# Turning expert and mix rows by VectorE in 32x32 blocks, from block-ordered loads, instead of by TensorE

## The chip, the core and the metric

The kernel runs on one core of one Trainium2 chip. A core has TensorE (PE, matrix products; its weight loads are shown as PEld), VectorE (DVE), ScalarE (ACT), GpSimd (POOL), SyncE (SP, which issues most DMAs here) and 16 DMA engines. The metric is the device time of one execution in microseconds, the median of the runs.

## What is computed

Input x has 4 sequences of 3072 rows of 256 numbers, 12288 rows (tokens) in all. Three stages follow one another:

```python
X = np.fft.fft(np.fft.fft(x, axis=1), axis=2).real        # 1. real part of a 2-D transform
x = X.reshape(12288, 256)

xn = x / (norm(x) + 1e-6); en = expert_emb / (norm(expert_emb) + 1e-6)
logits = xn @ en.T / tau                                   # 2. each row goes to one of 8 experts
e = argmax(logits); gate = softmax(logits)[e]
x = gate * (relu(x @ w1[e]) @ w2[e])                       # w1: 256x1024, w2: 1024x256

x_prev = x one row earlier in its sequence (zeros at its start)
xk = mu_k * x + (1 - mu_k) * x_prev; xr = mu_r * x + (1 - mu_r) * x_prev
k = relu(xk @ w_k)                                         # 3. mix; w_k: 256x1024
out = sigmoid(xr @ w_r) * ((k * k) @ w_v)                  # w_r: 256x256, w_v: 1024x256
```

## The kernel before

All matrix products of stages 2 and 3 run in three passes, since every operand is split into a high and a low part (`mm3`, L194): high by high, high by low, low by high. One product therefore shows three lines in the profile, L195, L196 and L197.

**Stage 1**, `transform_phase`, computes the transform and scatters each finished row to the DRAM tensor `xrows`, sorted by its expert: expert e owns rows from e * 12288 on. A row there is 272 numbers (1088 bytes): the 256 values, the token's number and its 8 logits. Stage 1 also works ahead on expert 0, whose first chunks are done there; a planner (`Plan`) orders that work by costs and due times. The change leaves stage 1 alone. At its end the rows of the first chunk of expert 1 are loaded already (`early_tiles`).

**Stage 2**, `expert_phase`, takes the rows of an expert in tiles of 128 rows and chunks of 4, 3, 3 and 3 tiles. It has 29 chunks: the last one of expert 0 (number `NP`) and four for each of experts 1 to 7. The loop over chunks is written out by hand; every engine runs its instructions in the order of the program and waits on semaphores. For chunk i the loop does this:

- `gather(i + 2)` (L1453) issues the row loads of the chunk after the next on SyncE, one DMA of 128 rows for each tile (`load_rows`, L235).
- `weigh(i)` lists the steps that give the gates and the destination of each row; these read the row tiles as they are loaded.
- For each of the 8 slices `fc` of the hidden layer: `first_layer(i, fc)` multiplies w1 by the turned rows (6 matmuls of 384 or 512 columns into one of two PSUM banks "a"), ScalarE evicts the high part (L1270), VectorE the low part (L1271, `hl`); then some weight splitting (L1177 on ScalarE, L1180 on VectorE; the wide weights of stage 3 at L1216 to L1242); then `second_layer(i - 1, fc)` for the chunk before (3 matmuls of 256 columns for each tile).
- At `fc == 3`, `transposes(i + 1)` (L1456) turns the next chunk's rows so that the 256 values lie on partitions: `transpose_chunk` (L1310) lets TensorE transpose each 128x128 block against the identity into PSUM (L1316), ScalarE copies the high part `th` (L1317), VectorE subtracts for the low part `tl` (L1318).
- At the end `finish(i - 1)` scales the chunk's results into tiles `y` (L1498) and GpSimd scatters them to the DRAM tensor `ydram` in token order (L178).

The loads of the raw weights, 1 MB each (`expert_raw`, L1164), go through the same SyncE queue.

**Stage 3**, `mix_phase`, runs over 24 blocks j of 512 tokens. `load(j)` (L1586) fetches a block from `ydram` with one DMA of 512 KB in runs of 1 KB, three buffers deep. `prepare(j + 1)` spreads the next block's preparation over the steps `fc` of block j: in steps 0 and 1 `turn(0)` and `turn(1)` (L1606) turn one half of the 256 values each (four TensorE transposes, L1609, and a ScalarE copy, L1610); in steps 2 to 6 `begin` and `end` form the two mixtures (L1617, L1618, L1624, L1625). Step fc of block j is, in this order: `key_layer(j, fc)` (6 matmuls of 512 columns, then L1661 on ScalarE and L1663 on VectorE); the second half of the previous step's squares (`late`: L1669 on ScalarE, L1670 `hl` on VectorE); a gate tile in steps 4 to 7; one step of `prepare`; and `value_layer` of two steps before (12 matmuls of 256 columns). When that was a block's last value layer, `finish` multiplies its four results in PSUM with the gates (L1701, `ot`, VectorE), which frees the four PSUM banks "b", and stores the block. So `finish(j - 1)` stands in step 1 of block j, behind `turn(1)`, and the value layer that opens the new block's sums in those banks stands in step 2.

At the start of stage 3 three blocks are loaded at once, while TensorE still does the second layer of the last chunk of stage 2.

Of the kernel before, what the change touches and what calls it, by code (L numbers as in the profile page):

```python
# [10 lines left out]
F32 = mybir.dt.float32  # L11
# [4 lines left out]
ACTF = mybir.ActivationFunctionType  # L16
ALU = mybir.AluOpType
# [4 lines left out]
D = 256  # L22
E = 8
F = 1024
NTOK = NB * S
# [20 lines left out]
NP = len(FIRST_CHUNKS) - 1  # L46
# [188 lines left out]
def load_rows(g, e, o, n, later=()):  # L235

    tiles = []
    for t in range(o, o + n):
        x = g.xg.tile([128, ROW], F32, tag="xg", name="xg")
        r = e * NTOK + 128 * t  # L240
        ins = g.nc.sync.dma_start(out=x, in_=g.xrows[r:r + 128]).ins
        for other in later:
            g.tc.declare_no_dep(ins, other, reason="rows of later ranks")
        g.row_reads.append(ins)
        tiles.append(x)
    return tiles
# [914 lines left out]
def expert_raw(g, e, n):  # L1161
    raw = g.xs.tile([128, 2048], F32, tag="xs", name="wraw")
    src = g.aps[n][e].rearrange("(k p) f -> p k f", p=128)
    g.nc.sync.dma_start(out=raw.rearrange("p (k f) -> p k f", k=src.shape[1]), in_=src)  # L1164
    return raw


def split_steps(g, raw, width=512, pool="w8"):

    nc = g.nc  # L1170
    hi, lo = [(g.w8 if pool == "w8" else g.xs).tile([128, 2048], F32R, tag=pool, name=n) for n in ("wh", "wl")]

    def piece(o):
        def fn():
            if o < 2048:
                s = slice(o, o + width)
                nc.scalar.activation(out=hi[:, s], in_=raw[:, s], func=ACTF.Copy)  # L1177
            if o:
                s = slice(o - width, o)
                nc.vector.tensor_tensor(out=lo[:, s], in0=raw[:, s], in1=hi[:, s].bitcast(F32), op=ALU.subtract)  # L1180
        return fn

    return (hi, lo), [piece(o) for o in range(0, 2049, width)]
# [123 lines left out]
    ]  # L1307


def transpose_chunk(g, tiles, ntile, dst_h, dst_l, tag="c"):  # L1310
    nc = g.nc
    for k in range(2):
        pt = g.ps.tile([128, 512], F32, tag=tag, bufs=g.banks[tag], name="pt")
        n = ntile * 128
        for t in range(ntile):
            nc.tensor.transpose(pt[:, t * 128:(t + 1) * 128], tiles[t][:, k * 128:(k + 1) * 128], g.ident)  # L1316
        nc.scalar.activation(out=dst_h[:, k, 0:n], in_=pt[:, 0:n], func=ACTF.Copy)  # L1317
        nc.vector.tensor_tensor(out=dst_l[:, k, 0:n], in0=pt[:, 0:n], in1=dst_h[:, k, 0:n].bitcast(F32),  # L1318
                                op=ALU.subtract)


def overflow_table(g, p2):
# [113 lines left out]
def expert_phase(g):  # L1436
    nc, tc = g.nc, g.tc
    a = g.aps
# [1 line left out]
    g.ps = g.ctx.enter_context(tc.tile_pool(name="ps", bufs=2, space=bass.MemoryType.PSUM))  # L1440
    g.banks = {"a": 2, "b": 4, "c": 2}
    xt_p = g.right.enter_context(tc.tile_pool(name="xt", bufs=2, side="right"))
    g.y = g.ctx.enter_context(tc.tile_pool(name="y", bufs=6))
    g.xs = g.inner.enter_context(tc.tile_pool(name="xsp", bufs=3))
    p2 = ctx.enter_context(tc.tile_pool(name="p2", bufs=1))
    y_p = g.y
# [3 lines left out]
    allc = [(0, o, n) for o, n, _ in FIRST_CHUNKS] + [(e, o, n) for e in range(1, E) for o, n in CHUNKS]  # L1450
    tiles, xts = g.early_tiles, {NP: g.early_x}

    def gather(i):  # L1453
        tiles[i] = load_rows(g, *allc[i])

    def transposes(i):  # L1456
        n = allc[i][2]
        th = xt_p.tile([128, 2, 512], F32R, tag="th", name="th")
        tl = xt_p.tile([128, 2, 512], F32R, tag="tl", name="tl")
        transpose_chunk(g, tiles[i], n, th, tl)  # L1460
        xts[i] = th, tl

    w = {0: list(g.w_first)}
# [38 lines left out]
    raws[1, 0] = expert_raw(g, 1, "w1")  # L1502
    for i, n in enumerate(("mu_k", "mu_r")):
        nc.sync.dma_start(out=g.mu[:, i, :], in_=a[n].rearrange("(k p) -> p k", p=128))
    for i in range(NP, n_all - 1):
        e, o, n = allc[i]
        if i == NP + 2:
            g.m2, wide = wide_weight_steps(g, cv_p)
        if i == NP + 1:
            overflow_table(g, p2)  # L1510
            nc.vector.tensor_scalar(out=g.omu, in0=g.mu, scalar1=-1.0, scalar2=1.0, op0=ALU.mult, op1=ALU.add)
        if i + 2 < n_all:
            gather(i + 2)

        c = (i - NP - 1) % len(CHUNKS) if e else 1
        if c == 0:
            second, fill = split_steps(g, raws[e, 1], pool="w8" if e + 1 < E else "xs")
            w[e].append(second)
            if e + 1 < E:
                raws[e + 1, 0] = expert_raw(g, e + 1, "w1")  # L1520
        if c == 1 and e + 1 < E:
            raws[e + 1, 1] = expert_raw(g, e + 1, "w2")
            first, fill = split_steps(g, raws[e + 1, 0])
            w[e + 1] = [first]
        weigh(i)
        for fc in range(8):
            first_layer(i, fc)
            for _ in range(-(-len(weighs) // (8 - fc))):
                weighs.pop(0)()
            if fc in (1, 3, 5, 6, 7) and fill:  # L1530
                fill.pop(0)()
            for _ in range(1 + (fc % 3 == 0)):
                if wide:
                    wide.pop(0)()
            if i > NP:
                second_layer(i - 1, fc)
            if fc == 3 and i + 1 < n_all:
                transposes(i + 1)
        if i > NP:
            finish(i - 1)  # L1540
# [32 lines left out]
def mix_phase(g):  # L1573
    nc, tc = g.nc, g.tc
    a = g.aps
    ctx = g.right
    yl_p = ctx.enter_context(tc.tile_pool(name="yl", bufs=3, side="right"))
# [6 lines left out]
    ld, yts, mixed = {}, {}, {}  # L1584

    def load(j):  # L1586
        t = yl_p.tile([128, 4, D], F32, tag="yl", name="yl")
        nc.sync.dma_start(out=t, in_=g.ydram[j * 512:(j + 1) * 512].rearrange("(t p) d -> p t d", p=128))
        ld[j] = t

    def prepare(j):

        yt = yt_p.tile([128, 2, 516], F32, tag="yt", name="yt")
        t = ld.pop(j)
        yts[j] = yt
        prev = yts.pop(j - 1, None)
        res = [[mx_p.tile([128, 2, 512], F32R, tag=f"m{q}{m}", name="mix") for q in range(2)] for m in range(2)]
        mixed[j] = res

        def halo():  # L1600
            if j % (S // 512) == 0:
                nc.vector.memset(yt[:, :, 3:4], 0.0)
            else:
                nc.vector.tensor_copy(out=yt[:, :, 3:4], in_=prev[:, :, 515:516])

        def turn(k):  # L1606
            pt = g.ps.tile([128, 512], F32, tag="c", bufs=2, name="pt")
            for s in range(4):
                nc.tensor.transpose(pt[:, s * 128:(s + 1) * 128], t[:, s, k * 128:(k + 1) * 128], g.ident)  # L1609
            nc.scalar.activation(out=yt[:, k, 4:516], in_=pt, func=ACTF.Copy)  # L1610

        tms = {}

        def begin(m, k):
            tm = mx_p.tile([128, 512], F32, tag="tm", name="tm")
            tms[m, k] = tm
            nc.scalar.activation(out=tm, in_=yt[:, k, 3:515], func=ACTF.Copy, scale=omu[:, m, k:k + 1])  # L1617
            nc.vector.scalar_tensor_tensor(out=tm, in0=yt[:, k, 4:516], scalar=mu[:, m, k:k + 1],  # L1618
                                           in1=tm, op0=ALU.mult, op1=ALU.add)

        def end(m, k):
            hi, lo = res[m]
            tm = tms.pop((m, k))
            nc.scalar.activation(out=hi[:, k], in_=tm, func=ACTF.Copy)  # L1624
            nc.vector.tensor_tensor(out=lo[:, k], in0=tm, in1=hi[:, k].bitcast(F32), op=ALU.subtract)  # L1625

        qs = [(0, 0), (0, 1), (1, 0), (1, 1)]

        def slot(i):
            def fn():  # L1630
                if i == 0:
                    halo()
                if i < 2:
                    turn(i)
                if 3 <= i < 7:
                    end(*qs[i - 3])
                if 2 <= i < 6:
                    begin(*qs[i - 2])
            return fn

        if j:
            return [slot(i) for i in range(7)]
        return [
            lambda: (halo(), turn(0)),
            lambda: (begin(*qs[0]), turn(1)),
            lambda: (end(*qs[0]), begin(*qs[1])),
            lambda: (end(*qs[1]), begin(*qs[2])),
            lambda: (end(*qs[2]), begin(*qs[3])),
            lambda: end(*qs[3]),
        ]  # L1650
# [54 lines left out]
    for j in range(3):  # L1705
        load(j)
# [5 lines left out]
    for at in range(8 * NBLK):  # L1712
        j, fc = divmod(at, 8)
# [12 lines left out]
        if at >= LAG:  # L1726
            k, kc = divmod(at - LAG, 8)
# [160 lines left out]
```

## Time and profile before

| | before |
|---|---|
| median of 3 runs (lowest to highest) | 1419.52 us (1418.83 to 1420.88) |
| profiled execution: its time, and its span | 1421.69 us, 1419.9 us |
| TensorE (PE) busy | 1357.0 us, 96% |
| weight loads (PEld) busy | 1268.2 us, 89% |
| VectorE (DVE) busy | 833.8 us, 59% |
| ScalarE (ACT) busy | 757.0 us, 53% |
| GpSimd (POOL) busy | 278.9 us, 20% |
| DMA | 75947 packets, 105.12 MB, mean 74 GB/s |

The page of the profile cuts the span into 40 equal slices of 35.5 us and gives each engine's busy share in tenths (9 is 90% or more):

```profile
PE   4768998999999999999999999999999999999998
DVE  8685346555555555554332666666666666666664
ACT  2445545545455555455544665566565565565563
PEclk9879999999999999999999999999999999999999
DMA  9843336123213131322102111110010111110000
```

The first six or seven slices are stage 1, the next fifteen stage 2 (from about 230 us), the rest stage 3 (from about 775 us). PEclk is the clock granted to TensorE, in tenths of full speed. Matmuls are pipelined, so their durations overlap: what one costs in a stream is seen from the distance between starts, not from its duration. In the timeline, a line's bracket holds the idle time of its engine just before it and who ended it.

### The profile page before, as it was taken

How to read it: one execution, taken by the hardware profiler on the slowest of the kernel's cores; microseconds unless marked ns; L12 is line 12 of the kernel's file. 1: busy time of each engine (PE TensorE's matmuls, PEld its weight loads, DVE VectorE, ACT ScalarE, POOL GpSimd, SP SyncE). 2: the span in 40 equal slices, each digit the busy share in tenths (PEclk: the TensorE clock that was granted, in tenths of full speed). 3: DMA queues.
4: the chain of work that ended last, by engine and by line, in shares of the span. 5: the costliest groups of instructions: out<-in, count | busy, mean ns of one | idle time of the engine just before them, and what ended most of it. 6: DMA issues, size and time to landing. Idle time of an engine off the chain costs nothing. (4 is left out here: it accounts for less than half of the span.)

```text
span 1419.9 us, 24364 instructions
## 1 busy us (share of the span) xinstructions
PE 1357.0 (96%) x9252; PEld 1268.2 (89%) x9252; DVE 833.8 (59%) x1905; ACT 757.0 (53%) x1888; POOL 278.9 (20%) x275
## 2 busy tenths in 40 slices
PE   4768998999999999999999999999999999999998
PEld 3657897999999999999999899999999999999998
DVE  8685346555555555554332666666666666666664
ACT  2445545545455555455544665566565565565563
POOL 5677673122222221222221000000000000000000
PEclk9879999999999999999999999999999999999999
DMA  9843336123213131322102111110010111110000
GB/s 287 195 132 111 115 108 196 69 80 108 80 62 126 53 99 57 98 76 80 47 23 68 39 60 31 30 60 30 31 60 30 44 47 30 56 35 31 30 16 30
DMA packets 75947, 105.12 MB, mean 74 GB/s; under 512 B 7694, under 2 KB 65331, under 8 KB 75188
## 3 DMA queue, kind: packets, MB, share of 16 engines
q1 hardware_dynamic: 61148, 72.74, 16.2%
q0 software_dynamic: 14352, 30.69, 7.1%
q8 instruction: 73, 1.20, 0.4%
q14 instruction: 46, 0.38, 0.1%
q10 hardware_dynamic: 328, 0.12, 0.0%
HBM read 62.73 MB, written 41.81 MB: 74 GB/s over the span
## 5 line engine op out<-in xcount | busy, mean ns | idle before, releaser
L1271 DVE SCALAR_TENSOR_TENSOR hl<-ph,hh 128x384 fp32r<-128x384 f32 (+1 forms) x232 | 136.6, 590 | 238.3 <-ACT hh L1270 237.2
L1663 DVE SCALAR_TENSOR_TENSOR k<-ph,r 128x512 f32<-128x512 f32 x192 | 132.8, 692 | 221.0 <-ACT r L1661 221.0
L1661 ACT ACTIVATE r<-ph 128x512 f32<-128x512 f32 x192 | 114.9, 598 | 257.4 <-PE ph L197 257.4
L1270 ACT ACTIVATE hh<-ph 128x384 fp32r<-128x384 f32 (+1 forms) x232 | 119.9, 517 | 238.9 <-PE ph L197 238.8
L195 PE MATMUL po<-wv,hh 128*128 128x256 f32 x768 | 219.6, 286 | 0.7 <-ACT hh L1669 0.7
L197 PE MATMUL po<-wv,hl 128*128 128x256 f32 x768 | 216.8, 282 | 0.4 <-DVE hl L1670 0.4
L196 PE MATMUL po<-wv,hh 128*128 128x256 f32 x768 | 215.3, 280 | 0.0
L195 PE MATMUL po<-wh,hh 128*128 128x256 f32 x752 | 211.4, 281 | 2.0 <-DVEq L1380 2.0
L197 PE MATMUL po<-wh,hl 128*128 128x256 f32 x752 | 211.0, 281 | 0.0
L196 PE MATMUL po<-wl,hh 128*128 128x256 f32 x752 | 210.6, 280 | 0.0
L178 POOL DMA_INDIRECT ydram<-y,ids x94 | 94.8, 1008 | 409.9 <-DVE ids L264 263.4
L195 PE MATMUL ph<-th,wh 128*128 128x384 f32 (+1 forms) x448 | 158.9, 355 | 0.7 <-DVE hl L1271 0.6
L197 PE MATMUL ph<-th,wl 128*128 128x384 f32 (+1 forms) x448 | 157.1, 351 | 0.0
L196 PE MATMUL ph<-tl,wh 128*128 128x384 f32 (+1 forms) x448 | 156.7, 350 | 0.0
L195 PE MATMUL ph<-mix,wk 128*128 128x512 f32 x384 | 151.7, 395 | 0.0
L196 PE MATMUL ph<-mix,wk 128*128 128x512 f32 x384 | 151.5, 394 | 0.0
L197 PE MATMUL ph<-mix,wk 128*128 128x512 f32 x384 | 151.4, 394 | 0.0
L195 PEld LDWEIGHTS po<-wv,hh 128*128 128x128 f32 x768 | 144.4, 188 | 3.2 <-ACT hh L1669 0.9
L196 PEld LDWEIGHTS po<-wv,hh 128*128 128x128 f32 x768 | 144.7, 188 | 2.2
L195 PEld LDWEIGHTS po<-wh,hh 128*128 128x128 f32 x752 | 142.1, 189 | 4.7 <-issue 2.3
L197 PEld LDWEIGHTS po<-wv,hl 128*128 128x128 f32 x768 | 144.5, 188 | 0.6 <-DVE hl L1670 0.6
L196 PEld LDWEIGHTS po<-wl,hh 128*128 128x128 f32 x752 | 142.3, 189 | 2.7
(262 smaller groups left out, 2974.8 us busy)
## 6 DMA issues: line engine op xcount, KB each, us to landing
wraw<-in_w_dram SPq DMA_DIRECT2D x16, 1024.0 KB
xg<-xrows SPq DMA_DIRECT2D x104, 136.0 KB
yl<-ydram SPq DMA_DIRECT2D x24, 512.0 KB
out_dram<-ot SPq DMA_DIRECT2D x23, 512.0 KB
xs<-in_xg_dram SPq DMA_DIRECT2D x9, 512.0 KB
xs<-in_xg_dram POOLq DMA_DIRECT2D x9, 512.0 KB, 7.4
xs<-in_xg_dram SPq DMA_DIRECT2D x3, 1024.0 KB
xrows<-zero SPq DMA_DIRECT2D x2, 1088.0 KB
```

The source lines that it names most:

```text
L178: ins = g.nc.gpsimd.indirect_dma_start(in_offset=None, oob_is_err=False, **kw).ins
L195: nc.tensor.matmul(out=out, lhsT=ah, rhs=bh, start=first, stop=False)
L196: nc.tensor.matmul(out=out, lhsT=ah, rhs=bl, start=False, stop=False)
L197: nc.tensor.matmul(out=out, lhsT=al, rhs=bh, start=False, stop=last)
L1270: return (lambda: nc.scalar.activation(out=hh[:, 0:N], in_=ps[:, 0:N], func=ACTF.Relu), lambda: nc.vector.scalar_tensor_tensor(out=hl[:, 0 ...
L1271: lambda: nc.vector.scalar_tensor_tensor(out=hl[:, 0:N], in0=ps[:, 0:N], scalar=0.0, in1=hh[:, 0:N].bitcast(F32), op0=ALU.max, op1=ALU.sub ...
L1661: nc.scalar.activation(out=r, in_=ps, func=ACTF.Relu)
L1663: nc.vector.scalar_tensor_tensor(out=k2, in0=ps, scalar=0.0, in1=r, op0=ALU.max, op1=ALU.mult)
```

## The change

Row loads for turning are made a second time, in the order of 32x32 blocks: `load_blocks` issues, for each half k of the 256 values and each group q of 32 partitions, one DMA on SyncE, whose runs are 32 numbers (128 bytes). Partition 32q + p of the result holds, for each group of 32 rows, 32 consecutive values of its p-th row; VectorE's transpose of 32x32 blocks then gives the turned rows at once. In stage 2 the old row loads stay, since gates and destinations are read from them; the blocks come beside them, into the new pool `xb` (two buffers, and one tile `xT` for the turned rows). The rows of chunk NP + 1, loaded in stage 1, get only their blocks, at the start of stage 2. ScalarE and VectorE then read `xT` in SBUF in place of PSUM. In stage 3 the block load takes the place of the old load, and VectorE's transpose takes the place of four TensorE transposes and a ScalarE copy. Expert 0's chunks, turned in stage 1, stay as they were. The pool `y` goes from six buffers to four.

```diff
-def transpose_chunk(g, tiles, ntile, dst_h, dst_l, tag="c"):
-    nc = g.nc
+def load_blocks(nc, out, rows):
+
+    n, step = rows.shape[0], rows.ap[0][0]
     for k in range(2):
-        pt = g.ps.tile([128, 512], F32, tag=tag, bufs=g.banks[tag], name="pt")
-        n = ntile * 128
-        for t in range(ntile):
-            nc.tensor.transpose(pt[:, t * 128:(t + 1) * 128], tiles[t][:, k * 128:(k + 1) * 128], g.ident)
-        nc.scalar.activation(out=dst_h[:, k, 0:n], in_=pt[:, 0:n], func=ACTF.Copy)
-        nc.vector.tensor_tensor(out=dst_l[:, k, 0:n], in0=pt[:, 0:n], in1=dst_h[:, k, 0:n].bitcast(F32),
-                                op=ALU.subtract)
+        for q in range(4):
+            src = bass.AP(rows.tensor, rows.offset + 128 * k + 32 * q, [[step, 32], [32 * step, n // 32], [1, 32]])
+            nc.sync.dma_start(out=out[32 * q:32 * q + 32, k, 0:n].rearrange("p (a j) -> p a j", j=32), in_=src)
 
@@ expert_phase
-    g.y = g.ctx.enter_context(tc.tile_pool(name="y", bufs=6))
+    xb_p = g.right.enter_context(tc.tile_pool(name="xb", bufs=2, side="right"))
+    g.y = g.ctx.enter_context(tc.tile_pool(name="y", bufs=4))
 
-    def gather(i):
-        tiles[i] = load_rows(g, *allc[i])
+    blocks = {}
+
+    def gather(i, here=False):
+        e, o, n = allc[i]
+        if not here:
+            tiles[i] = load_rows(g, e, o, n)
+        blocks[i] = xb_p.tile([128, 2, 512], F32, tag="xb", name="xb")
+        r = e * NTOK + 128 * o
+        load_blocks(nc, blocks[i], g.xrows[r:r + 128 * n, 0:D])
 
     def transposes(i):
-        n = allc[i][2]
+        N = allc[i][2] * 128
         th = xt_p.tile([128, 2, 512], F32R, tag="th", name="th")
         tl = xt_p.tile([128, 2, 512], F32R, tag="tl", name="tl")
-        transpose_chunk(g, tiles[i], n, th, tl)
+        x, xb = xb_p.tile([128, 2, 512], F32, tag="xT", bufs=1, name="xT"), blocks.pop(i)
+        for k in range(2):
+            nc.vector.transpose(out=x[:, k, 0:N], in_=xb[:, k, 0:N])
+            nc.scalar.activation(out=th[:, k, 0:N], in_=x[:, k, 0:N], func=ACTF.Copy)
+        for k in range(2):
+            nc.vector.tensor_tensor(out=tl[:, k, 0:N], in0=x[:, k, 0:N], in1=th[:, k, 0:N].bitcast(F32),
+                                    op=ALU.subtract)
         xts[i] = th, tl
 
@@ expert_phase, ahead of the loop over chunks
+    gather(NP + 1, True)
     for i in range(NP, n_all - 1):
 
@@ mix_phase
     def load(j):
-        t = yl_p.tile([128, 4, D], F32, tag="yl", name="yl")
-        nc.sync.dma_start(out=t, in_=g.ydram[j * 512:(j + 1) * 512].rearrange("(t p) d -> p t d", p=128))
+        t = yl_p.tile([128, 2, 512], F32, tag="yl", name="yl")
+        load_blocks(nc, t, g.ydram[j * 512:(j + 1) * 512])
         ld[j] = t
 
         def turn(k):
-            pt = g.ps.tile([128, 512], F32, tag="c", bufs=2, name="pt")
-            for s in range(4):
-                nc.tensor.transpose(pt[:, s * 128:(s + 1) * 128], t[:, s, k * 128:(k + 1) * 128], g.ident)
-            nc.scalar.activation(out=yt[:, k, 4:516], in_=pt, func=ACTF.Copy)
+            nc.vector.transpose(out=yt[:, k, 4:516], in_=t[:, k])
```

## Rows read from the trace of the kernel before

**Rows 1.** Windows: busy us (xcount) of each engine, TensorE clock, DMA share, GB/s.

```profile
265.00:490.00 225.00, 224.76 (x1580) 218.24 (x1579) 124.56 (x343) 116.81 (x346) 49.57 (x51) 1.00 0.26 83
...
800.00:1400.00 600.00, 600.00 (x4020) 548.28 (x4019) 390.29 (x663) 353.48 (x683) 0.00 (x0) 1.00 0.12 38
```

**Rows 2.** Lines view, TensorE transposes: xcount | busy us, mean ns | idle before.

```profile
L1609 PE MATMUL pt<-pack,yl 128*128 128x128 f32 x192 | 28.7, 271 | 0.0
...
L1316 PE MATMUL pt<-pack,xg 128*128 128x128 f32 x182 | 24.4, 272 | 0.0
```

**Rows 3.** Timeline, mix, without and with a group: start us, us, engine line.

```profile
1001.73 0.39 PE L197 MATMUL ph<-mix,wk 128*128 128x512 f32 x1
...
1002.08 0.28 PE L196 MATMUL po<-wv,hh 128*128 128x256 f32 x1
...
1021.49 0.39 PE L197 MATMUL ph<-mix,wk 128*128 128x512 f32 x1
1021.72 0.60 PE L1609 MATMUL pt<-pack,yl 128*128 128x128 f32 x4
...
1022.28 0.28 PE L196 MATMUL po<-wv,hh 128*128 128x256 f32 x1
```

**Rows 4.** Timeline, TensorE, expert chunk, without and with a group.

```profile
497.78 0.28 PE L197 MATMUL po<-wh,hl 128*128 128x256 f32 x1
...
498.07 0.34 PE L196 MATMUL ph<-tl,wh 128*128 128x384 f32 x1
...
500.23 0.28 PE L197 MATMUL po<-wh,hl 128*128 128x256 f32 x1
500.35 0.82 PE L1316 MATMUL pt<-pack,xg 128*128 128x128 f32 x6
...
501.18 0.34 PE L196 MATMUL ph<-tl,wh 128*128 128x384 f32 x1
```

**Rows 5.** Source view, VectorE, 1024 columns: duration ns min/median/max.

```profile
L455 DVE TENSOR_TENSOR xs<-xs x3: 1217/1225/1225, 33.3 to 95.4; 128x1024 f32<-128x1024 f32 x3
```

**Rows 6.** Lines view, VectorE, nearest shapes in SBUF.

```profile
L1625 DVE TENSOR_TENSOR mix<-tm,mix 128x512 fp32r<-128x512 f32 x96 | 66.4, 691 | 3.7 <-ACT mix L1624 2.1
...
L1222 DVE TENSOR_SCALAR fb<-ab 128x256 int32<-128x256 int32 x18 | 5.5, 305 | 0.0
```

**Rows 7.** Timeline, VectorE, mix, second step of a block.

```profile
1026.46 0.68 DVE L1670 TENSOR_TENSOR hl<-k,hh 128x512 fp32r<-128x512 f32 x1
1027.06 1.41 DVE L1701 TENSOR_TENSOR ot<-po,sg 128x256 f32<-128x256 f32 x4
```

**Rows 8.** Source view, VectorE, output products: duration ns min/median/max.

```profile
L1701 DVE TENSOR_TENSOR ot<-po,sg x96: 412/416/425, 817.0 to 1416.3; 128x256 f32<-128x256 f32 x96
```

**Rows 9.** Timeline, TensorE, mix, first value matmul of the next step.

```profile
1028.22 0.28 PE L195 MATMUL po<-wv,hh 128*128 128x256 f32 x1
```

**Rows 10.** Timeline, VectorE and TensorE, around one expert chunk's transposes.

```profile
500.94 0.29 DVE L1222 TENSOR_SCALAR fb<-ab 128x256 int32<-128x256 int32 x1
...
505.90 0.34 PE L195 MATMUL ph<-th,wh 128*128 128x384 f32 x1
```

**Rows 11.** Windows view: the first three mix loads, 1 KB runs.

```profile
775.00:780.00 5.00, 5.00 (x32) 5.00 (x32) 0.06 (x1) 1.19 (x3) 0.00 (x0) 0.66 0.91 303
```

**Rows 12.** Timeline, SyncE's queue, start of the expert phase.

```profile
230.58 1.80 SPq L241 DMA_DIRECT2D xg<-xrows  x3
```

**Rows 13.** Timeline, ScalarE and TensorE, start of the expert phase.

```profile
235.13 0.63 ACT L1177 ACTIVATE wh<-wraw 128x512 fp32r<-128x512 f32 x1 [1.82 <-DMA wraw<-in_w_dram]
...
240.30 0.44 PE L195 MATMUL ph<-xT,wfirst 128*128 128x384 f32 x1 [1.15 <-DVE hl L1271]
```

**Rows 14.** Timeline, SyncE, TensorE, ScalarE, start of the mix.

```profile
773.60 0.39 SPq L1588 DMA_DIRECT2D yl<-ydram  x1
...
774.13 0.38 PE L195 MATMUL po<-wh,hh 128*128 128x256 f32 x1 [1.99 <-DVEq L1380]
...
781.12 0.60 ACT L1610 ACTIVATE yt<-pt 128x512 f32<-128x512 f32 x1 [0.17 <-PE pt L1609]
```

## The prediction

> **What bounds the kernel now.** I read the windows view first, one stretch of the expert phase and one of the mix, to see which engine has no gap. In both it is TensorE: 224.76 of 225 us and 600.00 of 600 us busy at the full granted clock, where VectorE is busy 55% and 65% and the DMA engines 26% and 12% [rows 1]. So a microsecond of TensorE work that goes is a microsecond of the span, until another engine makes TensorE wait. Then the lines view, for what is to be removed: 192 transposes in the mix and 182 in the experts, with no idle time before them [rows 2]. Their mean of 271 ns is not their price, since matmuls overlap; the price comes from the distance between their neighbours' starts in the timeline.
>
> **Part 1, the transposes leave TensorE.** In the mix the last key matmul and the second value matmul behind it start 0.35 us apart without a group of four transposes (1001.73, 1002.08) and 0.79 us apart with one (1021.49, 1022.28): 0.44 us a group [rows 3]. There are 192/4 = 48 groups: 21.1 us. In an expert chunk of three tiles the same distance is 0.29 us without (497.78, 498.07) and 0.95 us with six (500.23, 501.18): 0.66 us, 0.11 each [rows 4]. Of the 182 I leave out the 8 of the first turned chunk, where TensorE waits for others anyway (part 4): 174 x 0.11 = 19.1 us. Together 40.2 us.
>
> **Part 2, the mix: VectorE turns.** ScalarE loses its copy out of PSUM, VectorE gets two 128x512 transposes a block. The trace has none, so its price is bounded by rows: at most the 1.22 us of a sum over twice the columns [rows 5], at least the 0.305 us of the cheap form over half of them. I take 0.69 us, the ordinary pass over 512 columns in SBUF [rows 6], which holds VectorE 0.60 us before the next starts [rows 7].
> The Trainium skill, VectorE: DVE Perf Modes, section The three transpose paths, gives 390 ns for TensorE and 311 ns for VectorE per 128x128 (bf16), and its rules for authors send a 128x128 transpose to TensorE. An estimate from that page, four times 311 ns for 512 columns, is 1.24 us, at the upper end above; in this trace TensorE pays 0.11 us in the stream instead of 390 ns, so the rule's comparison is still more against the change.
> Where does it stand? turn(0) falls into a step where VectorE waits anyway. turn(1) falls into the second step of a block, between hl and the four output products of the block before (L1701), which free the banks that the next block's first value matmul needs. In the profile ot starts at 1027.06 [rows 7] and its first quarter takes 0.416 us [rows 8]: done at 1027.48. The value matmul starts at 1028.22 [rows 9] and comes 0.44 us earlier once the transposes just ahead of it are gone: 1027.78. Cover 0.30 us; 0.05 of it, an estimate, goes to the signal between the engines. The transpose takes 0.60 us, and its four DMA waits (one for each group of partitions) I put at 0.10 (between 0 and 0.2). So TensorE waits 0.60 + 0.10 - 0.25 = 0.45 us in 22 blocks (those that hold both a finish and a turn): +9.9 us. At the lower end of the transpose (0.22 + 0.10 - 0.25) it is 1.6 us, at the upper (1.14 + 0.10 - 0.25) 21.8 us.
>
> **Part 3, expert chunks in their steady part: nothing.** VectorE gets two transposes more a chunk, and ScalarE's copies, the later eviction and its subtraction queue behind them. Cover: in the chunk shown VectorE is free at 501.23 [rows 10]; two turns, a copy, an eviction and its subtraction at 384 columns, each three quarters of 0.69 [rows 6], end 2.6 us later at 503.8; TensorE needs that bank at 505.90 less 0.66 = 505.24 [rows 4, 10]. 1.4 us are left; at the upper end of the transpose the cover is about used up, and then each chunk loses some tenths. y with four buffers instead of six still holds one chunk's tiles.
>
> **Part 4, the loads.** Each tile of 512 KB now comes in 4096 runs of 128 bytes, 256 a DMA engine, issued as 8 DMAs, beside the row loads that stay for the experts. The nearest row is the mix's first three loads in 1 KB runs: 5.0 us at a share of 0.91 for 1536 runs, 96 an engine: 47 ns each [rows 11]. An eighth of that, by bytes alone, is 6 ns. SyncE needs 0.39 to 0.60 us per DMA [rows 12, 14], which for its 32 runs an engine is 12 to 19 ns, so less can't arrive in a burst. I take 20 ns. Steady need: 13 tiles x 64 = 832 runs an engine per expert, 17 us (39 at 47 ns) beside 0.26 of some 75 us (225 us of rows 1 hold three experts); in the mix 5 us (12) of 25. SyncE's eight issues, about 4 us, are queued ahead of the weight loads and behind the output store; buffers come free one to two chunks ahead. Covered, cost 0.
> Not covered is the start of the experts. The first turned chunk's rows were loaded early; its blocks are issued only where the phase begins, behind 1 MB of weights, in the place where row loads stood at 230.58 [rows 12]. Those weights are there at 235.13 [rows 13]. The blocks follow: 256 x 0.020 = 5.1, 240.2; then the turn 0.69, ScalarE's copy 0.60, a subtraction 0.69 and the waiting eviction's subtraction, 384 columns, 0.5: 242.7. TensorE resumes at 240.30 [rows 13], so +2.4. Its gap then grows from 1.15 to 3.5 us. What a gap can do is seen at the mix: after 1.99 us idle [rows 14] the granted clock is 0.66 over the next 5 us, that is part of them at 1.2 GHz [rows 11], 1.7 us of work lost; I add these: +4.1. At 47 ns it is 2.4 + 6.9 + 1.7 = 11.0; at 6 ns about 0.
> At the start of the mix load(0) is issued at 773.60 and the second turned half is ready at 781.12 + 0.60 = 781.72, having waited 0.17 us for TensorE [rows 14], whose transposes stand behind value matmuls there: the load is not the last to come, by how much no row shows. Its runs take 5.1 us an engine instead of 32 x 0.047 = 1.5, so the half comes between 0 and 3.6 us later; I take 1.0, since the load goes out while TensorE still has work, and the 0.88 us of the first two groups is then not felt: +1.9. At 47 ns (12.0 instead of 5.1) +8.8.
>
> **Sum.** The profiled execution took 1421.69 us, 2.17 above the median. 1421.7 - 40.2 + 9.9 + 4.1 + 1.9 = 1397.4; less 2.2, 1395 us beside a median of 1419.5.
>
> **Rivals.** (a) Nothing of parts 2 and 4 is felt: 1421.7 - 40.2 - 2.2 = 1379. For it: VectorE idles a third of the mix; against: that idle time isn't ahead of ot. (b) The transpose takes 1.22 us: 9.9 becomes 21.8, 1407. For it: nothing in the trace shows its speed. (c) A 128-byte run costs what 1 KB does: 6.9 more at either start, 1409. (d) Both (b) and (c): 1421, no change. (e) Slower: the DMA engines become the bound. Expert phase: 832 runs x t + 20 us exceed 75.5 - 2.9 = 72.6 from t = 63 ns on (mix: from about 90). At t = 75 ns an expert takes 82 us, 7 x 9.4 = 66 us more, and the starts 14 each: 1489. Against it: 47 ns for eight times the bytes. The Trainium skill, DMA: Bandwidth & Descriptors, section Specifications, speaks for (c) and (e): full rate needs 512 bytes, below it a read-modify-write is done. No row here shows that. (f) That a transpose stays on TensorE can't be, outside expert 0: no such instruction is left in the diff.
>
> **How the numbers follow.** Forecast 53%, (a) 12, (b) 10, (c) 9, (d) 6, (e) 10. The range goes from (a), 1379, to just past (b) and (c), 1412, and leaves out (d) and (e). A measurement here tells 0.2% from no change: faster is the forecast, (a), (b), (c), 84%; same (d), 6%; slower (e), 10%.
>
> **What would show it.** No TensorE transposes behind the start of the experts; mix blocks 0.4 us shorter, not 0.9, with one TensorE wait a block on ot at L1701's place; a VectorE transpose near 0.69 us; expert chunks shorter by 0.11 us a transpose; one gap of some 3.5 us in the first chunk. The forecast is wrong if the turn waits for its DMAs in the steady part, if the ot wait is absent, or if the transpose is far from 0.69 us.

## The result, and the profile after

The changed kernel takes 1397.53 us (median of 4 runs, 1396.48 to 1398.58) where the kernel before takes 1420.17 on the same chip: a ratio of 0.9842, 95% interval 0.9825 to 0.9859. The forecast was 1395, range 1379 to 1412. Its profiled execution took 1397.23 us, span 1395.5.

First the page: busy time of each engine, and the first DMA queue (packets, MB, share of 16 engines).

```profile
PE 1322.6 (95%) x8878; PEld 1227.9 (88%) x8878; DVE 887.7 (64%) x2009; ACT 734.1 (53%) x1840; POOL 277.0 (20%) x275
...
q1 hardware_dynamic: 246620, 84.69, 25.1%
```

TensorE works 34 us less and the span is 24 us shorter; the difference is new waiting. Where it is not, the windows view shows (columns as in [rows 1]):

```profile
265.00:490.00 225.00, 224.86 (x1564) 218.34 (x1564) 141.17 (x385) 123.32 (x363) 54.37 (x55) 1.00 0.43 114
...
800.00:1280.00 480.00, 474.84 (x3109) 428.90 (x3110) 337.76 (x576) 270.93 (x521) 0.00 (x0) 1.00 0.20 43
```

The steady experts stay without a gap, though the DMA engines went from a share of 0.26 to 0.43. The mix, without a gap in [rows 1], now has 5.2 us of them in 480. The waits view of TensorE from 790 to 1395 us (total us, times, longest) names their cause, and it is the only one there:

```profile
PE po L195 <- DVE ot L1710: 6.2, 22, 0.5
```

The new instruction in the lines view of VectorE (xcount | busy, mean ns | idle before), and for the experts in the source view (min/median/max ns):

```profile
L1619 DVE STREAM_TRANSPOSE yt<-yl 128x512 f32<-128x512 f32 x48 | 33.8, 705 | 2.8 <-DMA yl<-ydram 2.8
```
```profile
L1467 DVE STREAM_TRANSPOSE xT<-xb x56: 532/570/712, 236.6 to 730.1; 128x384 f32<-128x384 f32 x42, 128x512 f32<-128x512 f32 x14
```

One 128x512 transpose takes 0.705 us, about what the ordinary pass of [rows 6] takes. One wait in front of it is long, at the first mix block.

The place in the loop, in the timeline: VectorE and then TensorE, step 1 into step 2 of a mix block (compare [rows 7, 3]).

```profile
1006.06 0.68 DVE L1679 TENSOR_TENSOR hl<-k,hh 128x512 fp32r<-128x512 f32 x1
1006.66 0.70 DVE L1619 STREAM_TRANSPOSE yt<-yl 128x512 f32<-128x512 f32 x1
1007.29 1.38 DVE L1710 TENSOR_TENSOR ot<-po,sg 128x256 f32<-128x256 f32 x4
```
```profile
1007.16 0.40 PE L197 MATMUL ph<-mix,wk 128*128 128x512 f32 x1
1007.82 0.36 PE L195 MATMUL po<-wv,hh 128*128 128x256 f32 x1 [0.27 <-DVE ot L1710]
1008.02 0.28 PE L196 MATMUL po<-wv,hh 128*128 128x256 f32 x1
```

The transpose sits between hl and the four products and holds VectorE for 0.63 us (1006.66 to 1007.29). From the last key matmul to the second value matmul it is now 0.86 us instead of the 0.35 of [rows 3]. What a block takes is seen at its store; the first and the twentieth store on SyncE's queue, of the kernel before and then of the changed one:

```profile
818.47 0.38 SPq L1703 DMA_DIRECT2D out_dram<-ot  x1
...
1317.29 0.38 SPq L1703 DMA_DIRECT2D out_dram<-ot  x1
```
```profile
800.94 0.41 SPq L1712 DMA_DIRECT2D out_dram<-ot  x1
...
1293.96 0.40 SPq L1712 DMA_DIRECT2D out_dram<-ot  x1
```

Over 19 blocks that is 26.254 us a block before and 25.948 after: 0.305 less, not the 0.88 of two groups of transposes.

The start of the experts, in the timeline of SyncE, ScalarE, VectorE and TensorE (compare [rows 12, 13]):

```profile
227.40 0.38 SPq L1164 DMA_DIRECT2D wraw<-in_w_dram  x1
...
228.88 7.62 SPq L1316 DMA_DIRECT2D xb<-xrows  x8
```
```profile
236.60 0.71 DVE L1467 STREAM_TRANSPOSE xT<-xb 128x512 f32<-128x512 f32 x1 [0.40 <-DMA xb<-xrows]
238.64 0.71 DVE L1467 STREAM_TRANSPOSE xT<-xb 128x512 f32<-128x512 f32 x1 [1.33 <-DMA xb<-xrows]
...
241.27 0.69 PE L195 MATMUL ph<-xT,wfirst 128*128 128x384 f32 x1 [3.96 <-DVE hl L1271]
...
244.81 0.42 PE L195 MATMUL ph<-th,wh 128*128 128x512 f32 x1
```

The gap that was 1.15 us is 3.96 us; its releaser hl stands on VectorE behind the two transposes, which waited for their blocks, and the two subtractions `tl`.

Cut into stretches, the two traces say: from the first matmul of the chunk `NP`, behind a wait of 0.75 us on ScalarE in both (229.71 before, 228.08 after), to the first turned chunk's first matmul (242.80, 244.81) +3.64 us; from there to the mix's first load (773.60, 756.54) -19.07; from there to the end -7.34. Together -22.8, beside -22.6 of the medians. Ahead of the first stretch the profiled execution was also 1.63 us earlier, in work that the change doesn't touch.

### The profile page after: what moved, and what is told of

The parts are those of the page before. It is cut to its first block, busy times and chain, and to the rows that moved or that the text cites. A ratio compares the mean times of both kernels' runs of the same rounds, so it can differ in the third digit from the quotient of the medians.

```text
span 1395.5 us, 24153 instructions
## 1 busy us (share of the span) xinstructions
PE 1322.6 (95%) x8878; PEld 1227.9 (88%) x8878; DVE 887.7 (64%) x2009; ACT 734.1 (53%) x1840; POOL 277.0 (20%) x275
## 3 DMA queue, kind: packets, MB, share of 16 engines
q8 instruction: 70, 1.15, 0.3%
```

## The experiments

My theory: the mix loses the 0.575 us a block (0.88 less 0.305) because turn(1) is queued ahead of the products ot, and the start of the experts loses its 3.6 us because the block loads come late. The rivals: the loads in 128-byte runs cost this time, or VectorE's greater load as such.

**1. Both transposes in step 0.**

```diff
-                if i < 2:
-                    turn(i)
+                if i == 0:
+                    turn(0)
+                    turn(1)
```

> Both transposes of a mix block stand in step 0 of the block before it; step 1, where the four products ot of the block before are made, has none. Theory A (what the mix still loses is the second transpose, which stands on VectorE ahead of the four products that TensorE waits for): the wait of TensorE on ot, some 0.5 us in 22 blocks, goes, a block falls from 25.95 to about 25.4 us, and the time from 1397.5 to about 1386 us. Theory B (the loss comes from the loads in runs of 128 bytes, or from VectorE's larger load as such): both are as they were, so the block stays within 0.1 us of 25.95 and the time within 2 us of 1397.5.

Measured: 1389.46 us, ratio 0.9784 (0.9766 to 0.9801). The wait on ot is gone from the waits view. SyncE's first and twentieth store, then VectorE and TensorE where the 0.86 us stood:

```profile
803.87 0.40 SPq L1713 DMA_DIRECT2D out_dram<-ot  x1
...
1287.11 0.39 SPq L1713 DMA_DIRECT2D out_dram<-ot  x1
```
```profile
1005.35 0.68 DVE L1680 TENSOR_TENSOR hl<-k,hh 128x512 fp32r<-128x512 f32 x1
1005.95 1.41 DVE L1711 TENSOR_TENSOR ot<-po,sg 128x256 f32<-128x256 f32 x4
...
1006.45 0.42 PE L197 MATMUL ph<-mix,wk 128*128 128x512 f32 x1
1006.70 0.29 PE L195 MATMUL po<-wv,hh 128*128 128x256 f32 x1
1006.82 0.28 PE L196 MATMUL po<-wv,hh 128*128 128x256 f32 x1
```

25.434 us a block, 0.514 less, and 0.37 us from matmul to matmul: theory A. The whole time fell by 8 us rather than the 11 expected; the profiled execution was 1.32 us later ahead of the first stretch, and lost more at the two starts: 17.47 us against 16.73 in the first stretch, where its code is the changed kernel's and the granted clock was 0.74 against 0.90, and 45.28 against 44.40 from the mix's first load to its first store. Beside experiment 2 the same edit gave 10.9 us (experiment 3).

**2. The first turned chunk on TensorE.**

```diff
     def transposes(i):
...
+        if i == NP + 1:
+            transpose_chunk(g, tiles[i], allc[i][2], th, tl)
+            xts[i] = th, tl
+            return
...
-    gather(NP + 1, True)
```

> The first turned chunk alone (the first of expert 1) is turned by TensorE from the rows loaded early, as in the kernel before; its eight block loads fall out. Theory A (the gap of 3.96 us in the first chunk is the wait for these late block loads): the gap shrinks to the 1.15 us that the kernel before had, and the time falls by about 3.6 us to 1394. Theory B (the gap comes from VectorE and ScalarE being busy with the norms, weights and hl there, whoever turns the rows): the gap stays near 4 us and the eight transposes come on top, 1397.5 to 1398.5 us.

Measured: 1392.71 us, ratio 0.9813 (0.9799 to 0.9828), 4.8 us under the changed kernel. TensorE in the timeline:

```profile
236.78 0.44 PE L195 MATMUL ph<-xT,wfirst 128*128 128x384 f32 x1 [1.15 <-DVE hl L1271]
...
239.27 0.50 PE L195 MATMUL ph<-th,wh 128*128 128x512 f32 x1
```

The gap is the 1.15 us of before, the first matmul behind it is at full clock (0.44 us where it was 0.69), and the stretch takes 12.77 us instead of 16.73. Theory A.

**3. Both edits.**

> Both edits at once: both transposes in step 0 of a mix block, and the first turned chunk of the experts turned by TensorE. Theory A (the two losses are separate and both are what the forecast named): about 1397.5 - 11.5 - 3.6 = 1382.5 us. Theory B (each loss has another cause, the loads or VectorE's load): within 3 us of 1397.5. If only one of the two falls, 1386 or 1394 us.

Measured: 1381.80 us, ratio 0.9735 (0.9721 to 0.9749); 25.423 us a block, 12.85 us in the first stretch. The losses are separate and both are what was named. This version beats both kernels.

**4. The experts alone, 5. the mix alone.** Experiment 4 puts the mix's row load and TensorE transposes back:

```diff
-        load_blocks(nc, t, g.ydram[j * 512:(j + 1) * 512])
+        nc.sync.dma_start(out=t, in_=g.ydram[j * 512:(j + 1) * 512].rearrange("(t p) d -> p t d", p=128))
...
-            nc.vector.transpose(out=yt[:, k, 4:516], in_=t[:, k])
+            pt = g.ps.tile([128, 512], F32, tag="c", bufs=2, name="pt")
+            for s in range(4):
+                nc.tensor.transpose(pt[:, s * 128:(s + 1) * 128], t[:, s, k * 128:(k + 1) * 128], g.ident)
+            nc.scalar.activation(out=yt[:, k, 4:516], in_=pt, func=ACTF.Copy)
```

> The experts as in the changed kernel, the mix as in the kernel before (row loads, transposes on TensorE, ScalarE moves them out of PSUM). Theory A (the parts add up as the two traces show by stretch: -19.1 us in the steady experts, +3.6 us at their start, about -7.4 us in the mix): 1420.2 - 15.5 = about 1404.7 us, with the mix blocks back at 26.25 us. Theory B (the expert part's true gain is smaller and the mix part brings more, because a stretch of the trace ends where a queue ends and not where TensorE does): 1408 us or more.

Experiment 5 makes the opposite edit on the kernel before: only the mix loads blocks and turns on VectorE.

> The mix as in the changed kernel, the experts as in the kernel before (no block loads, transposes on TensorE). Theory A (the parts are separate and add up): the mix alone saves what the two traces show for its stretches, 0.5 us at the start, 0.305 us in each of some 20 blocks and 1 us at the end, 7.5 us, so 0.9947 times the kernel before (1412.5 us where that takes 1420); a block takes 25.95 us and the experts from their first turned chunk to the mix take what they took before. Theory B (the experts' loads and the mix share something, so that the mix alone gains the full 0.88 us a block): 25.4 us a block, 0.985 times before.

Measured: the experts alone 1404.84 us, ratio 0.9892 (0.9875 to 0.9909), blocks back at 26.274 us. The mix alone 1413.34 us, ratio 0.9950 (0.9937 to 0.9962), blocks at 25.934. The ratios leave 15.3 and 7.1 us of gain, 22.4 together, which is the whole. Theory A in both: the parts add up. One term of experiment 5's forecast missed: from the mix's first load to its first store it took 45.68 us, 0.8 more than the kernel before and not 0.5 less (on the clock there, see experiment 8).

**6. The block loads twice.** Experiments 1 to 4 ran on the chip that the record numbers 11, the others on number 9. While 6 to 9 ran, every kernel there, the one before too (1474.96 us), took some 55 us more, nearly all of it ahead of the experts. Why is open: beside experiments 5 and 10 the kernel before took 1419.97 us on number 9. The times of 6 to 9 are read as ratios to the kernel before, and the mix by its stretches, which agree with those of the changed kernel's trace.

```diff
+        if j >= 3:
+            spare = yl_p.tile([128, 2, 512], F32, tag="spare", bufs=1, name="spare")
+            load_blocks(nc, spare, g.ydram[j * 512:(j + 1) * 512])
```

> Each mix block from the fourth on is loaded twice, the second time into a buffer that nobody reads: 21 times 4096 more runs of 128 bytes. Theory A (the loads are covered, a run costs a DMA engine some 14 ns): the time stays within 1.5 us of 1397.5, the first queue gets 21 x 4096 x 14 ns = 1.2 ms more of engine time, 5.4% of 16 engines' span. Theory B (the block loads are part of what the mix loses, by contention or on SP's queue): at least half of the 0.575 us a block comes once more, 1403 us or more.

Measured: ratio 0.9879 (0.9843 to 0.9915), too wide to decide by itself. The trace decides: 25.947 us a block against 25.948, and 638.90 us from the mix's first load to the end against 638.96. The loads are covered, theory A by the blocks; by the time it isn't decided. And the price of a run can be read: the first queue in the window 860 to 1340 us of this kernel, and of experiment 8, which loads once:

```profile
q1 hardware_dynamic: 170524, 29.88, 33.1%
```
```profile
q1 hardware_dynamic: 89778, 19.42, 19.0%
```

(0.331 - 0.190) x 16 x 480 us over 80,746 packets is 13.4 ns for a 128-byte run.

**7. A spare transpose in step 1, 8. in step 3.**

```diff
+                if i == 1 and j > 1:
+                    junk = mx_p.tile([128, 512], F32, tag="junk", bufs=1, name="junk")
+                    nc.vector.transpose(out=junk, in_=t[:, 0])
                 if i < 2:
                     turn(i)
```

> A second transpose, into a buffer that nobody reads, stands ahead of the second transpose of a mix block, in step 1, from the third block on (22 times). Theory A (whatever stands there on VectorE ahead of the four products comes in full onto TensorE's path): 0.63 us more for each, 22 x 0.63 = 14 us, 1411 us. Theory B (VectorE has slack there, the wait is for something else): less than 3 us, below 1400.5.

> The same spare transpose in step 3 of a block (22 times), where VectorE has also a product and a difference of the mix. Theory A (only step 1 is on the path; elsewhere some 0.63 us of VectorE are covered): within 1.5 us of 1397.5. Theory B (VectorE's load as such costs time, by the chain through k and hl to TensorE): at least 5 us more, 1402 or above.

Measured: in step 1 the ratio is 0.9939 (0.9917 to 0.9962) where the changed kernel had 0.9842. A block takes 26.547 us, 0.599 more, and from the mix's first load to the end it is 653.54 us against 638.96, 14.6 more. The waits view of TensorE from 860 us to 1370 us:

```profile
PE po L195 <- DVE ot L1713: 17.5, 20, 1.1
```

In step 3 (`i == 3` in the diff) a block takes 25.947 us, 0.001 less. The ratio, 0.9877 (0.9842 to 0.9911), lies as wide and as high as in experiment 6, whose mix lost nothing; the stretch from the mix's first load to the end took 1.4 us more than in the changed kernel, all of it at its start, where the first spare transposes aren't made yet. There the granted clock differs (third number from the end): over the first 11 us it is 1.00 in the changed kernel and 0.84 here, as it is in experiments 1, 5 and 7.

```profile
756.00:767.00 11.00, 9.79 (x77) 9.49 (x78) 4.77 (x9) 4.82 (x7) 0.00 (x0) 1.00 0.63 100
```
```profile
811.00:822.00 11.00, 9.67 (x68) 9.67 (x69) 4.86 (x9) 4.82 (x7) 0.00 (x0) 0.84 0.62 99
```

So by the blocks it is theory A both times: 0.63 us of VectorE costs 0.60 in step 1 and nothing in step 3.

**9. The first chunk's block loads ahead of the weights.**

```diff
+    gather(NP + 1, True)
     raws[1, 0] = expert_raw(g, 1, "w1")
...
-    gather(NP + 1, True)
```

> The eight block loads of the first turned chunk are issued ahead of the 1 MB weight load of expert 1 instead of behind it (some 1.5 us earlier on SP's queue, and with nothing of theirs behind the weights' packets). Theory A (the gap of 3.96 us is the wait for block loads that stand behind the weights): the blocks land some 3 us earlier, the gap shrinks to 1 to 2 us, and the time falls by 2 to 3 us to about 1395. Theory B (the gap moves on to the weights, which now come 4 us later and are split for expert 1 in the same stretch): no gain, 1397 to 1399 us, with ScalarE or VectorE waiting for the weights there. Theory C (the loads cost their own eight issues, wherever they stand): a gain of no more than the 1.5 us.

Measured: ratio 0.9838 (0.9802 to 0.9873), which can't be told from 0.9842. In the timeline SyncE issues the blocks seven us ahead of the weights, since the weight load waits 2.6 us for a matmul; ScalarE's first copy of a weight, VectorE's transposes and TensorE around its last two gaps, then the window in which it resumes (clock is the third number from the end):

```profile
285.91 0.63 ACT L1177 ACTIVATE wh<-wraw 128x512 fp32r<-128x512 f32 x1 [1.84 <-DMA wraw<-in_w_dram]
...
287.56 0.44 PE L195 MATMUL ph<-xT,wfirst 128*128 128x384 f32 x1 [1.93 <-DVE hl L1271]
...
288.37 0.35 PE L196 MATMUL ph<-xT,wfirst 128*128 128x384 f32 x1
288.54 0.49 PE L197 MATMUL ph<-xT,wfirst 128*128 128x384 f32 x1
288.75 1.30 DVE L1467 STREAM_TRANSPOSE xT<-xb 128x512 f32<-128x512 f32 x2
...
291.98 0.69 PE L195 MATMUL ph<-xT,wfirst 128*128 128x384 f32 x1 [1.02 <-DVE hl L1271]
```
```profile
289.00:295.00 6.00, 4.98 (x16) 4.47 (x15) 4.05 (x8) 3.76 (x11) 0.00 (x0) 0.50 0.80 218
```

The transposes wait for nothing, the gap is 1.02 us and the weights come no later (ScalarE waits 1.84 us for them, 1.82 in [rows 13]): on the gap theory A is right, B is out. But the granted clock was 0.50 here. It fell ahead of that gap and not behind it: from 288.54 on, 1 us after TensorE resumed from the idle of 1.93 us, the matmuls up to the gap take 0.49 to 0.53 us, where the one before took 0.35. The stretch still took 15.27 us at a mean clock of 0.78, against 15.02 (1.00), 16.90 (0.84) and 17.56 (0.83) in experiments 6, 7 and 8, which load late. The gap is shown; that closing it in this way pays in time is not, and theory C's small gain can't be told from none.

**10. Three edits.** Experiment 2; turn(1) in step 2, behind the products; the first mix block's eight loads from two queues:

```diff
+            eng = nc.scalar if two and q % 2 else nc.sync
...
-                if i < 2:
-                    turn(i)
+                if i in (0, 2):
+                    turn(i // 2)
```

> Three edits on the changed kernel: the first turned chunk of the experts on TensorE; the second transpose of a mix block in step 2, behind the four products, instead of step 1; the eight loads of the first mix block issued from two queues, half by SP and half by ScalarE. Theory A (step 2 is as free as step 0, and the start of the mix hangs on the issue of the first block's loads, for which VectorE waited 2.81 us): 25.43 us a block as with both transposes in step 0, the wait of VectorE falls below 1.5 us, and the time is 1 to 1.5 us under that of the kernel with both turns in step 0 and the first chunk on TensorE, 0.9725 times before. Theory B (the start of the mix is bound by ScalarE's and VectorE's chain behind the loads, and ScalarE now also issues): no gain, 0.9735 times before or more.

Measured: 1382.16 us, ratio 0.9727 (0.9714 to 0.9740), not to be told from experiment 3. Step 2 is as free as step 0 (25.428 us a block). VectorE's wait for the first mix block did not shrink:

```profile
758.33 0.71 DVE L1635 STREAM_TRANSPOSE yt<-yl 128x512 f32<-128x512 f32 x1 [3.31 <-DMA yl<-ydram]
```

It was 2.81 us in the changed kernel. Of theory A the first half holds, the second fell: the eight issues alone don't set that wait. Nor does the 3.31 show that it grew: over the nine traces that issue this block from SyncE alone the wait is 2.54 to 3.37 us. What does set it stays open. The DMA share there is 1.16 and 1.42 over two windows of 3 us, where experiment 3 has at most 0.79, so contention may have a part; that isn't shown apart.

## Why the prediction was right

**Part 1 held.** 174 transposes x 0.11 us was 19.1 us; the steady experts gave 19.07. For the mix 0.88 us a block; with the wait out of the way (experiments 1, 3, 10) it is 0.82 to 0.83; the 0.05 that is missing no run explains.

**Part 2 was the right mechanism and was sized a little too small.** Forecast: 0.60 + 0.10 - 0.25 = 0.45 us in 22 blocks, 9.9 us. Measured: 22 waits, and 0.51 to 0.53 us a block by experiments 1 and 3, so some 11.5 us. By terms: the transpose holds VectorE 0.63 us, not 0.60; the wait for its DMAs, put at 0.10, isn't there; the cover is less, since TensorE started 0.12 us after the first quarter of ot was done (1007.29 + 0.41 = 1007.70, then 1007.82), where I gave the signal 0.05, and experiment 1 has 0.34 us between those two: 0.22 of cover. And the first matmul after a wait costs some 0.08 more (0.20 us to the next, 0.12 in experiment 1), which I had not counted. 0.63 - 0.22 + 0.08 = 0.49, so the 0.10 that isn't there made up for most of what was sized too small: that 0.45 came so near is in part luck. Rival (b), a transpose of 1.22 us, fell with the 0.705. The Trainium skill, VectorE: DVE Perf Modes, section The three transpose paths, led to an estimate of 1.24 us; the trace has 0.705. The same page's rule (section Rules for kernel authors) that TensorE is the place for a 128x128 transpose does not carry over either: here TensorE is the bound, the blocks are put in order by the loads, and experiment 3 ends 38 us below the kernel before.

**Part 3 held.** No wait on blocks and no gap in the steady experts.

**Part 4: covered where I said, and the run cheaper than taken.** 20 ns was forecast, bounds 6 and 47; it is 13.4 (experiment 6). Rivals (c), (d) and (e) fall with it. A 1 KB run takes 47 ns [rows 11], so a short run is cheaper by 3.5 times and dearer by the byte, 2.3 times. By that, what the Trainium skill states in DMA: Bandwidth & Descriptors, section Specifications, that line rate needs 512 bytes, agrees in direction; no run here shows the read-modify-write it gives as the reason.

Start of the experts, forecast +2.4 for the gap and +1.7 for the clock, 4.1; measured +3.64. The gap grew by 2.81. The matmuls at lower clock (241.27 to 244.81, 3.54 us against 2.50) cost 1.04. The gap ahead of it grew from 1.01 to 1.68. And the eight transposes that I left out do give 0.87: with the gaps taken off, 229.71 to 240.30 is 8.25 us of work before and 7.38 after. 2.81 + 1.04 + 0.67 - 0.87 is 3.65. The last two nearly cancel, and leaving the eight out was sound: in the kernel before they filled part of a wait for the weights. TensorE resumed, counted from the first matmul, 13.19 us on, where the forecast has 242.7 - 229.71 = 13.0. That is in part luck: at 13.4 ns the 256 runs of an engine are 3.4 us instead of 5.1, but SyncE took 7.62 us over the eight issues, put at about 4, and the last ended at 236.50, 2.1 us ahead of the second transpose.

Start of the mix: with +1.9, one stall of 0.45 and six groups less (2.64) the forecast says -0.3 up to the first store; it is -0.47 (44.87 to 44.40). Its place was right in kind: VectorE's first turn waits 2.81 us for the load. But the same code took 45.68 us in experiment 5, where the clock was lower, so one trace doesn't confirm a term of this size.

**The sum.** 40.2 less of 9.9 + 4.1 + 1.9 was to save 24.3 us; by stretches it is 22.8. The mix is 2.0 us worse than forecast, mostly the stall, the start of the experts 0.5 better. That the profiled execution met 1397.4 almost exactly is chance: 1.6 us of it come from stage 1. The medians, 22.6 us apart, are the better measure.

## What to carry to other kernels

When an operation leaves the engine that bounds the kernel, look at the queue it joins: not that engine's busy share, but what stands behind the new instruction in program order and who waits for that. The same 0.63 us cost 0.60 a block in one step and nothing two steps later, so moving one line gave back 0.51 us of the 0.575 lost. The loop may hide a load completely and the phase's first load not at all: price first iterations by themselves, and keep the old way for them if its data is already there.

## What was not expected of the hardware

- A 32x32-block transpose on VectorE, fp32 from SBUF to SBUF, costs what an ordinary pass does: 0.705 us for 512 columns, some 0.57 for 384.
- A run of 128 bytes from DRAM costs a DMA engine 13.4 ns (experiment 6 against 8). Experiment 6 puts the engines in the mix at a share of 0.34 without a tenth of a us on a block.
- The length of the gap just ahead doesn't settle what the clock does. The first matmul behind it took 0.69 us (half clock, 1.2 GHz) after 3.96 us here, but 0.44 (full, 2.4 GHz) after 3.51 in experiment 6. In experiments 1 and 9 the clock fell during work, about 1 us after TensorE had resumed from idles of 1.88 and 1.93 us; after one of 1.89 in experiment 4 it did not. What else decides is open.
- At the start of the mix the same code ran at full clock for its first 11 us in the changed kernel and at a mean of 0.84 in experiments 5 and 8.
- One of the eight block loads took SyncE 3.4 us to issue, where the median is 0.47; this happened while the 1 MB weight load was under way.
